# QK projection of a gated attention block: the gate's sums in another tile, raw x of the second pass loaded in other pieces, and folded router weights and u in one scratch

## The chip, the cores and the metric

The kernel runs on one core of a Trainium2 chip. Five engines work side by side, each through its own list of instructions: TensorE (PE) multiplies matrices into the banks of PSUM, ScalarE (ACT) and VectorE (DVE) read those banks and SBUF, GpSimd (POOL) does small work, and SyncE (SP) issues DMAs. SP, ACT and POOL each issue DMAs through a queue of their own. An instruction that waits holds everything behind it on its engine. The metric is the device time of one execution in microseconds, median of several runs.

## The reference, cut to what matters

`x` is 2048 tokens of 1024 features. Multi-head attention (32 heads of 32) and a sparse layer of 64 experts, chosen with two tables of 8 keys each, are mixed by a gate per token:

```python
x = A_x
g = _sigmoid((x * gate_w).sum(-1, keepdims=True))
a = _A_ref(x, A_wqkv, A_wo)      # qkv = x @ wqkv, softmax attention, @ wo
b = _B_ref(x, B_w_q, B_k1, B_k2, B_u, B_v)
return g * a + (1 - g) * b
...
# in _B_ref
q = jnp.einsum("nd,dhc->nhc", xf, w_q)
s1 = jnp.einsum("nhd,ed->nhe", q[..., :dk], k1)      # s2 with q[..., dk:] and k2
...
act = _gelu(jnp.einsum("nd,nhkd->nhk", xf, ue))      # ue = u of the best key pair
out = jnp.einsum("nhk,nhk,nhkd->nd", g, act, ve)
```

All is float32.

## The kernel before, in words

**Numbers in two parts.** Each float32 operand of a matmul is split in a rounded part *hi* (a copy on ScalarE, `hi_of`, line 135) and the rest *lo* (a subtraction on VectorE, `lo_of`, line 138). A product takes three matmuls for each 128 features: hi by hi, hi by lo, lo by hi.

**The QK projection** computes the q and k columns of `x @ wqkv` in 16 units, each with 128 columns of q and 128 of k for 1024 tokens. Pass 1 (units 0 to 7) takes tokens 1024 to 2047, pass 2 (units 8 to 15) tokens 0 to 1023, with the column chunks in reversed order, so unit 8 uses the chunk of unit 7. Half of the features (index 1 or 2) by half of the tokens makes quarters B11, B12, B21, B22 of x and A11, A12, A21, A22 of the weights. Units 0 and 8 are plain: four banks, each with 8 feature chunks by three matmuls (`plain_mm`, matmuls at line 279). The other units use Strassen's scheme with 7 products in place of 8 (`product`, line 291): P1, P5, P6, P2, P7, P3, P4 in this order, each of 12 matmuls. They need sums of quarters: T1 to T4 of x (`x_sum`, line 152, once for each pass, made in the place of a raw quarter), S1 to S4 of the weights (`w_sum`, line 222, for every unit). VectorE adds the products to the results (line 492), and `evac` turns each result, or each plain bank, into hi and lo, stores both to DRAM by DMAs on ScalarE's queue, and has ScalarE sum squares (line 245). The squares read the bank in place and come last, so they are what frees it.

**Order.** The program is written in the order of issue for each engine. Between the products, `hook(name)` runs what the table `hooks[unit, name]` holds, and `ready(name)` prepares the next unit's weights; PE's order is that of the calls. A product takes the next of six banks in turn.

**The gate.** `gate_mm` (line 190) multiplies raw x with `gate_w` into one bank; `gate_out` copies four rows of it (line 196) to the tile `zs` and sends them to DRAM, with POOL's DMAs. `zs` was a corner of the tile `rb` that also holds raw B22, and hi and lo of T3 take the slot of that tile in pass 1 (xh2) and pass 2 (xl2).

**The fold.** The router's scores are linear in x, so `w_q` is multiplied with differences of the keys once: `fold` (matmuls at line 330, two steps after most units, `wqt` being loaded pieces of `w_q`), a copy of the finished bank (line 335), then four transposes `fold_t` (line 347), a copy to the tile u7 (line 350) and a POOL DMA into the DRAM scratch WPD: 448 columns of router weights for each of 8 feature chunks.

**Pass 2's x and the router's weights.** Raw x of pass 2 is loaded by SP in units 6 and 7: B21 to the tile x8 and, as 4 pieces of 512 KB, B11 with B12 to `ra`, then B22 to `rb`. In units 14 and 15 `open_rw` reads WPD back into eight tiles wpl, and u (64 more columns) into `ugr`; `split_wp` splits them by chunk in 448 and 64 columns, and `split_n1` splits one more quarter of x, whose tile the router's own x loads (rx, on SP) follow. Then the router runs for 16 tiles of 128 tokens (24 matmuls each at line 704, a copy xu at line 708, a chain of small operations on VectorE at lines 712 to 746, eq on POOL at line 718), after it the values of attention (Strassen products at line 927), attention itself and the output.

## Time and profile before

| | |
|---|---|
| median of 3 runs | 1872.17 us (1870.14 to 1874.34) |
| profiled execution | 1873.74 us, span 1872.0 us |
| mean granted clock of PE | 0.991 |
| PE busy | 1830.5 us (98%) |
| VectorE busy | 1459.0 us (78%) |
| ScalarE busy | 1314.8 us (70%) |
| POOL busy | 174.3 us (9%) |

The span is what the profiler saw of one execution; 1.74 us of the time lie outside it. A row of a timeline gives start, duration, engine, line, operation, output<-inputs, shape and count, and in brackets the idle time of the engine ahead of it with what ended that. A row of the waits gives who waited for whom, us in total, how often and the longest. In the windows' rows the figure after POOL is the granted clock of PE, the next one the DMA share. From about 660 us to the end the kernel is attention and output, which the change leaves alone.

### The profile page before, as it was taken

How to read it: one execution, taken by the hardware profiler on the slowest of the kernel's cores; microseconds unless marked ns; L12 is line 12 of the kernel's file. 1: busy time of each engine (PE TensorE's matmuls, PEld its weight loads, DVE VectorE, ACT ScalarE, POOL GpSimd, SP SyncE). 2: the span in 40 equal slices, each digit the busy share in tenths (PEclk: the TensorE clock that was granted, in tenths of full speed). 3: DMA queues.
4: the chain of work that ended last, by engine and by line, in shares of the span. 5: the costliest groups of instructions: out<-in, count | busy, mean ns of one | idle time of the engine just before them, and what ended most of it. 6: DMA issues, size and time to landing. Idle time of an engine off the chain costs nothing.

```text
span 1872.0 us, 26493 instructions
## 1 busy us (share of the span) xinstructions
PE 1830.5 (98%) x10083; PEld 1107.3 (59%) x10083; DVE 1459.0 (78%) x1272; ACT 1314.8 (70%) x1730; POOL 174.3 (9%) x229
## 2 busy tenths in 40 slices
...
GB/s 248 203 278 248 219 208 279 252 151 177 29 118 242 231 199 169 159 181 154 179 161 183 169 173 174 170 179 164 185 170 182 151 177 171 180 158 177 286 182 57
DMA packets 136978, 344.99 MB, mean 184 GB/s; under 512 B 18320, under 2 KB 60080, under 8 KB 117712
## 3 DMA queue, kind: packets, MB, share of 16 engines
...
## 4 chain that ended last, share of the span: by engine, by line
PE 60%; issue 7%; DMA 4%; DVE 2%; POOL 2%; ACT 0%; SPq 0%; DVEq 0%; ACTq 0%; POOLq 0%
PE ring L1281 27%; PE o L1302 25%; PE pa L927 6%; PE ring L1315 1%; POOL eq L718 1%; DMA accd<-P 1%; DMA accd<-rd 1%; DMA out<-rb 1%; PE pa L1493 1%; DMA smd<-ssb 1%; SPq L76 0%; DMA t1l<-xl 0%; DVE eq L728 0%; DVE mm L725 0%; DMA V<-od 0%
## 5 line engine op out<-in xcount | busy, mean ns | idle before, releaser
L1291 ACT ACTIVATE P<-ring 128x1024 f32<-128x1024 f32 (+2 forms) x1031 | 912.9, 985 | 13.8 <-DMA accd<-P 1.0
L1331 DVE TENSOR_TENSOR acc<-acc,P 128x2048 f32<-128x2048 f32 x319 | 730.9, 2291 | 74.9 <-ACT P L1291 49.6
L1302 PE MATMUL o<-P,V 128*32 128x512 f32 x3840 | 464.8, 599 | 0.0
L1281 PE MATMUL ring<-Q,K 98*128 98x512 f32 x1024 | 272.0, 407 | 0.2
L1281 PE MATMUL ring<-z,z 98*128 98x512 f32 x1020 | 270.5, 407 | 0.6 <-ACT accd L1291 0.6
L1281 PEld LDWEIGHTS ring<-Q,K 98*128 98x128 f32 x1024 | 181.9, 188 | 144.4 <-ACT P L1291 72.6
L1281 PEld LDWEIGHTS ring<-z,z 98*128 98x128 f32 x1020 | 181.4, 188 | 142.5 <-ACT P L1291 72.4
L1302 PEld LDWEIGHTS o<-P,V 128*32 128x32 f32 x3840 | 98.8, 109 | 223.3 <-issue 214.2
L1324 POOL DMA_DIRECT2D accd<-P x95 | 81.5, 858 | 930.1 <-ACT P L1291 419.8
L1329 DVE TENSOR_TENSOR acc<-P,P 128x2048 f32<-128x2048 f32 x32 | 73.4, 2292 | 72.8 <-ACT P L1291 72.8
L291 PE MATMUL bk<-xh,S 128*128 128x512 f32 x336 | 83.2, 401 | 1.9 <-ACT bk L245 1.9
L291 PE MATMUL bk<-xh,A 128*128 128x512 f32 x336 | 82.8, 396 | 0.0
L291 PE MATMUL bk<-xl,S 128*128 128x512 f32 x336 | 82.4, 398 | 0.0
L291 PEld LDWEIGHTS bk<-xh,A 128*128 128x128 f32 x336 | 62.0, 188 | 23.8 <-issue 9.2
L291 PEld LDWEIGHTS bk<-xh,S 128*128 128x128 f32 x336 | 64.7, 194 | 16.9 <-ACT bk L245 2.4
L135 ACT ACTIVATE hi<-u 128x512 fp32r<-128x512 f32 x42 | 26.5, 632 | 68.6 <-DVE u L492 65.3
L1334 DVE TENSOR_TENSOR acc<-acc,accd 128x2048 f32<-128x2048 f32 x32 | 73.1, 2285 | 0.0
L291 PEld LDWEIGHTS bk<-xl,S 128*128 128x128 f32 x336 | 63.8, 192 | 15.4 <-issue 1.7
L1291 ACT ACTIVATE accd<-ring 128x1024 f32<-128x1024 f32 (+2 forms) x64 | 62.3, 1033 | 2.3 <-PE ring L1281 2.2
L927 PE MATMUL pa<-woh,acc 128*128 128x512 f32 x192 | 62.2, 389 | 0.0
L138 DVE TENSOR_TENSOR A<-wraw,A 128x512 fp32r<-128x512 f32 x42 | 28.9, 688 | 32.8 <-ACT A L135 32.8
L291 PE MATMUL bk<-xl,A 128*128 128x512 f32 x168 | 44.5, 417 | 8.7 <-ACT A L135 4.4
...
## 6 DMA issues: line engine op xcount, KB each, us to landing
...
```

Source lines behind the costliest of these rows:

```text
L135: nc.scalar.activation(parts[0], src, AF.Copy)
L138: nc.vector.tensor_tensor(out=parts[1], in0=src, in1=parts[0].bitcast(F32), op=OP.subtract)
L291: nc.tensor.matmul(ps, a[i][:, k, :], b[j][:, k, :], start=(k == 0 and i == j == 0), stop=(k == HC - 1 and i == 1))
L718: nc.gpsimd.tensor_tensor(out=eq, in0=eq, in1=ranks.rearrange("p c a i e -> p (c a i) e"), op=OP.mult)
L927: nc.tensor.matmul(ps, self.a[a][i][:, k, :], self.b[b][j][k], start=(not first and k == 0 and i == j == 0), stop=(k == HC - 1 and i == 1))
L1281: on_ring(nc.tensor.matmul(ring[:, i, :], K[:98, kt * 128:(kt + 1) * 128], Q[:98, qc * 512:(qc + 1) * 512], start=True, stop=True), i)
L1291: on_ring(nc.scalar.activation(P[h, kt][:, q0 * 512:(q0 + m) * 512].rearrange("p (a m) -> p a m", a=m), ring[:, i:i + m, :], AF.Exp, scale ...
L1302: nc.tensor.matmul(O[h][32 * qc:32 * qc + 32, :], Vt[g][:, kt, 32 * j:32 * j + 32], p[:, qc * 512:(qc + 1) * 512], start=(kt == 0), stop=( ...
L1324: nc.gpsimd.dma_start(ACCD[h], P[h, kt], accum_op=OP.add)
L1329: nc.vector.tensor_add(ACC[h], P[h, 0], P[h, kt])
L1331: nc.vector.tensor_add(ACC[h], ACC[h], P[h, kt])
L1334: nc.vector.tensor_add(ACC[h], ACC[h], ACCD[h])
```

## The change

1. The gate's copies go to a 128x512 tile of the pool `ev` (u2, which units use for sums), no longer to the corner of `rb`.
2. At the start of unit 1 and through unit 8, gate_out, the T4 sum, the splits of T3, T4, A12, S3, S4 and the evacuations of the plain banks stand in another order. `fold_t` moves from behind P1 to behind P5 in every unit.
3. Pass 2's raw B11 goes to x8 at (6, P5); B21 and B12 come as two loads of 1 MB into `ra` at (7, P1). hi B11 follows at (7, P6). T4 of pass 2 is made in T1's place.
4. WPD gets rows of 512 columns. A POOL DMA at the start of the program copies u (1024 rows of 64) from DRAM to its last 64 columns. `open_rw` moves to (15, P1) and loads two halves of 1 MB; the splits are two of 2048 columns on each of ScalarE and VectorE, at (15, P2) and (15, P7). `split_n1` moves behind unit 15.

ScalarE from the end of unit 0 into unit 1, before (xh_143 is the slot of `rb`, xh_407 is hi of T3 in the same slot, xh_477 hi of T4, A_421 hi of A12, S_428 and S_471 hi of S3 and S4, bk_181 to bk_184 the plain banks):

```order
L196 ACTIVATE xh_143<-bk_294 1x256 x4
L135 ACTIVATE xh_407<-xh_142 128x2048
L135 ACTIVATE A_421<-wraw 128x512
L135 ACTIVATE hi<-bk_182 128x512
L135 ACTIVATE S_428<-S_387 128x512
L496 ACTIVATE c_465<-bk_452 128x512
L245 ACTIVATE bk_182,sq<-bk_182 128x512
L76 DMA kdh<-hi 128x512
L76 DMA kdl<-lo 128x512
L135 ACTIVATE S_471<-wraw 128x512
L135 ACTIVATE hi<-bk_183 128x512
L135 ACTIVATE xh_477<-x_144 128x2048
```

and after (xh_428 is hi of T3, xh_444 of T4, A_411 of A12, S_438 and S_442 of S3 and S4, u_418 the new tile for the gate):

```order
L135 ACTIVATE A_411<-wraw 128x512
L135 ACTIVATE hi<-bk_182 128x512
L197 ACTIVATE u_418<-bk_295 1x256 x4
L135 ACTIVATE xh_428<-xh_142 128x2048
L135 ACTIVATE hi<-bk_183 128x512
L246 ACTIVATE bk_182,sq<-bk_182 128x512
L76 DMA kdh<-hi 128x512
L76 DMA kdl<-lo 128x512
L135 ACTIVATE S_438<-S_388 128x512
L135 ACTIVATE S_442<-wraw 128x512
L135 ACTIVATE xh_444<-x_144 128x2048
L502 ACTIVATE c_480<-bk_467 128x512
```

A12 and one bank's hi now stand ahead of the gate's copies and T3, the second bank's hi ahead of both S; S4 and T4 come before the second squares (not in these rows).

ScalarE from unit 8 into unit 9, before (xl_1633 is the slot of `rb`; xl_1881 hi of T3, S_1911 hi of S3, xh_1925 hi of T4, A_1952 hi of A12):

```order
L196 ACTIVATE xl_1633<-bk_1765 1x256 x4
L135 ACTIVATE xl_1881<-xh_1615 128x2048
L135 ACTIVATE hi<-bk_1754 128x512
L135 ACTIVATE S_1911<-S_1831 128x512
L135 ACTIVATE hi<-bk_1753 128x512
L245 ACTIVATE bk_1754,sq<-bk_1754 128x512
L76 DMA kdh<-hi 128x512
L76 DMA kdl<-lo 128x512
L135 ACTIVATE S_1923<-wraw 128x512
L135 ACTIVATE xh_1925<-x_1435 128x2048
L135 ACTIVATE A_1952<-wraw 128x512
L135 ACTIVATE hi<-bk_1755 128x512
```

and after (u_1873 is the tile for the gate, xl_1882 hi of T3, A_1948 hi of A12, xh_1953 hi of T4):

```order
L197 ACTIVATE u_1873<-bk_1765 1x256 x4
L135 ACTIVATE xl_1882<-xh_1609 128x2048
L135 ACTIVATE hi<-bk_1754 128x512
L135 ACTIVATE hi<-bk_1753 128x512
L246 ACTIVATE bk_1754,sq<-bk_1754 128x512
L76 DMA kdh<-hi 128x512
L76 DMA kdl<-lo 128x512
L135 ACTIVATE S_1920<-S_1831 128x512
L135 ACTIVATE A_1948<-wraw 128x512
L135 ACTIVATE S_1950<-wraw 128x512
L135 ACTIVATE xh_1953<-x_1457 128x2048
L135 ACTIVATE hi<-bk_1755 128x512
```

The second hi of a bank and the first squares move ahead of S3, and A12 ahead of S4 and T4.

VectorE in unit 15, before (wpl the loaded weights and then their lo, c and u the sums of the unit, xh_3234 the last split of x, `split_n1`):

```order
L138 TENSOR_TENSOR wpl_3121<-ugr,wph_3113 128x64
L138 TENSOR_TENSOR wpl_3122<-wpl_3122,wph_3114 128x448
L138 TENSOR_TENSOR wpl_3122<-ugr,wph_3114 128x64
L492 TENSOR_TENSOR u_3196<-c_3149,bk_3183 128x512
L492 TENSOR_TENSOR u_3197<-u_3196,bk_3162 128x512
L492 TENSOR_TENSOR c_3149<-c_3149,bk_3216 128x512
L138 TENSOR_TENSOR lo<-c_3149,hi 128x512
L95 TENSOR_TENSOR xh_3234<-x_2963,xh_3234 128x2048
L492 TENSOR_TENSOR u_3250<-u_3197,bk_3237 128x512
L492 TENSOR_TENSOR u_3196<-u_3196,bk_3237 128x512
```

and after:

```order
L498 TENSOR_TENSOR u_3161<-c_3119,bk_3148 128x512
L498 TENSOR_TENSOR u_3162<-u_3161,bk_3135 128x512
L498 TENSOR_TENSOR c_3119<-c_3119,bk_3165 128x512
L138 TENSOR_TENSOR lo<-c_3119,hi 128x512
L138 TENSOR_TENSOR wpl_3129<-wpl_3129,wph_3131 128x2048
L498 TENSOR_TENSOR u_3198<-u_3162,bk_3185 128x512
L498 TENSOR_TENSOR u_3161<-u_3161,bk_3185 128x512
L138 TENSOR_TENSOR lo<-u_3198,hi 128x512
L138 TENSOR_TENSOR wpl_3130<-wpl_3130,wph_3132 128x2048
L498 TENSOR_TENSOR u_3162<-u_3162,bk_3210 128x512
L138 TENSOR_TENSOR lo<-u_3162,hi 128x512
```

The first sums of the unit now stand ahead of the splits of the weights, which are two, and `split_n1` comes behind all of it (not in these rows).

The diff:

```diff
--- before.py
+++ after.py
@@ -49,7 +49,7 @@
     QKD = [[dram.tile([D, S], F32R, name=f"{n}d{part}") for part in "hl"] for n in "qk"]
     SHD = dram.tile([H, 2, S], F32R, name="shd")
     VD = [dram.tile([S, 512], F32, name=f"vd{i}") for i in range(2)]
-    WPD = dram.tile([128, KC, 448], F32, name="wpd")
+    WPD = dram.tile([128, KC, 512], F32, name="wpd")
     ATD = dram.tile([128, S], F32R, name="atd")
     OD = [dram.tile([128, S], F32, name=f"od{g}") for g in range(G)]
     ZD = dram.tile([1, S], F32, name="zd")
@@ -147,7 +147,7 @@
     def x_sum(p, name):
 
         a, b = dict(T1=("B12", "B11"), T3=("B22", "B12"), T2=("B22", "T1"), T4=("B21", "T2"))[name]
-        out = dict(T1="B11", T3="B12", T2="B22", T4="B21")[name]
+        out = dict(T1="B11", T3="B12", T2="B22", T4="T1" if p else "B21")[name]
         XR[name] = XR[out]
         nc.vector.tensor_tensor(out=XR[name], in0=XR[a], in1=XR[b], op=OP.subtract)
 
@@ -159,12 +159,12 @@
 
         if which == "ra":
             ra = xp.tile([128, HC, 1024], F32, name=PASS[p]["ra"])
-            XR.update(ra=ra, B11=ra[:, :, :512], B12=ra[:, :, 512:])
+            XR.update({"ra": ra, "B21" if p else "B11": ra[:, :, :512], "B12": ra[:, :, 512:]})
         elif which == "rb":
             rb = xp.tile([128, KC * 512], F32, name=PASS[p]["rb"])
-            XR.update(B22=rb[:, :2048].rearrange("p (k m) -> p k m", k=HC), zs=rb[:, 2048:2304])
+            XR["B22"] = rb[:, :2048].rearrange("p (k m) -> p k m", k=HC)
         else:
-            XR["B21"] = x8.tile([128, HC, 512], F32, name="x8")
+            XR[which] = x8.tile([128, HC, 512], F32, name="x8")
 
     def load_x(p, kc, pieces=1):
         rows, t0 = slice(kc * 128, (kc + 1) * 128), TOK0[p]
@@ -191,11 +191,12 @@
                                  start=(kc == 0), stop=(kc == KC - 1))
 
     def gate_out(p):
+        zs = ev.tile([128, 512], F32, name="u2", bufs=1)
         for q in range(4):
             row = slice(32 * q, 32 * q + 1)
-            nc.scalar.activation(XR["zs"][row, :], pz[0][row, :256], AF.Copy)
+            nc.scalar.activation(zs[row, :256], pz[0][row, :256], AF.Copy)
             c = TOK0[p] + 256 * q
-            dma(ZD[:, c:c + 256], XR["zs"][row, :], nc.gpsimd)
+            dma(ZD[:, c:c + 256], zs[row, :256], nc.gpsimd)
 
 
     def load_w(u):
@@ -372,7 +373,7 @@
             hi, lo = X[f"B{ki + 1}{n + 1}"]
             split(hi[:, k, :], lo[:, k, :], XR[f"B{ki + 1}{n + 1}"][:, k, :])
 
-    for which in ("ra", "rb", "r21"):
+    for which in ("ra", "rb", "B21"):
         x_raw_tiles(0, which)
     for name in PLAIN.values():
         w_place(name)
@@ -396,6 +397,7 @@
     for i in range(11):
         nc.tensor.matmul(b0[1, 1][:, :128], ident, ident, start=True, stop=True)
     dma(gw, ug.rearrange("p (k m) -> p k m", k=KC)[:, :, 64:65], nc.gpsimd)
+    dma(WPD[:, :, 448:], ug.rearrange("p (k m) -> p k m", k=KC)[:, :, :64], nc.gpsimd)
     dma(kraw, k12.rearrange("p (a e) -> p a e", a=2), nc.gpsimd)
     kpad_diffs()
 
@@ -432,9 +434,6 @@
             w_hi(1, "S2")
             w_lo(1, "S2")
             x_lo(0, "T2")
-            gate_out(0)
-            x_sum(0, "T4")
-            x_hi(0, "T3")
         order = [(n, i) for i in range(3) for n in range(2)]
         if kc in (0, KC - 1):
             order = [(n, i) for n in range(2) for i in range(3)]
@@ -447,15 +446,22 @@
         evac(w, CHUNK[u], TOK0[u // KC] // 512 + n, b0[w, n], b0[w, n])
 
     hooks = {}
-    w_parts(1, "A12")
+    w_hi(1, "A12")
+    w_lo(1, "A12")
     plain_evac(0, 1, 0)
+    gate_out(0)
+    x_sum(0, "T4")
+    x_hi(0, "T3")
+    x_lo(0, "T3")
+    plain_evac(0, 0, 1)
     w_hi(1, "S3")
-    x_lo(0, "T3")
+    w_sum(1, "S4")
     w_lo(1, "S3")
-    hooks[1, "P1"] = [(w_sum, 1, "S4"), (w_hi, 1, "S4"), (plain_evac, 0, 0, 1), (x_hi, 0, "T4"),
-                      (w_lo, 1, "S4")]
-    hooks[1, "P5"] = [(x_lo, 0, "T4"), (plain_evac, 0, 1, 1), (w_parts, 1, "A22")]
-    hooks[1, "P6"] = [(plain_evac, 0, 0, 0)]
+    w_hi(1, "S4")
+    x_hi(0, "T4")
+    w_lo(1, "S4")
+    hooks[1, "P1"] = [(x_lo, 0, "T4"), (plain_evac, 0, 1, 1)]
+    hooks[1, "P5"] = [(w_parts, 1, "A22"), (plain_evac, 0, 0, 0)]
     load_w(2)
     fold()
     FOLDS = {1, 2, 3, 4, 5, 6, 8, 9, 10, 11, 12, 13}
@@ -495,10 +501,10 @@
         c1 = place("c1")
         nc.scalar.activation(c1, p1, AF.Copy)
         run_late()
-        fold_t()
         hook("P1")
         ready("P1")
         p5 = product("P5")
+        fold_t()
         hook("P5")
         ready("P5")
         p6 = product("P6")
@@ -546,17 +552,20 @@
 
     def next_raw(which):
         x_raw_tiles(1, which)
-        if which == "ra":
-            for kc in range(HC):
-                load_x(1, kc)
+        if which == "B11":
+            load_quarter(0, 0, XR["B11"])
+        elif which == "ra":
+            load_quarter(0, 1, XR["B21"])
+            load_quarter(1, 0, XR["B12"])
         else:
-            load_quarter(0 if which == "r21" else 1, 1, XR["B21" if which == "r21" else "B22"])
+            load_quarter(1, 1, XR["B22"])
 
     hooks[2, "P1"] = [(w_parts, 2, "A22")]
-    hooks[6, "P1"] = [(next_raw, "r21"), (load_a21,)]
+    hooks[6, "P5"] = [(next_raw, "B11"), (load_a21,)]
     hooks[7, "P1"] = [(next_raw, "ra")]
     hooks[7, "P5"] = [(next_raw, "rb")]
-    hooks[7, "P2-"] = [(f, 1, name) for f, name in ((x_hi, "B11"), (x_lo, "B11"), (x_hi, "B21"))]
+    hooks[7, "P6"] = [(x_hi, 1, "B11")]
+    hooks[7, "P2-"] = [(x_lo, 1, "B11"), (x_hi, 1, "B21")]
     hooks[7, "P2"] = [(x_lo, 1, "B21")]
     hooks[7, "P7-"] = [(x_hi, 1, "B12")]
     hooks[7, "P7"] = [(x_lo, 1, "B12")]
@@ -589,8 +598,8 @@
     x_sum(1, "T2")
     w_lo(nxt, "S1")
     plain_group(0, 1)
+    x_hi(1, "T2")
     w_hi(nxt, "A11")
-    x_hi(1, "T2")
     x_sum(1, "T4")
     w_lo(nxt, "A11")
     w_sum(nxt, "S2")
@@ -601,19 +610,19 @@
     x_hi(1, "T3")
     plain_group(1, 0)
     plain_evac(KC, 1, 0)
+    x_lo(1, "T3")
+    plain_evac(KC, 0, 0)
     w_hi(nxt, "S3")
-    x_lo(1, "T3")
+    w_sum(nxt, "S4")
     w_lo(nxt, "S3")
-    plain_evac(KC, 0, 0)
-    w_sum(nxt, "S4")
+    plain_group(1, 1)
+    w_hi(nxt, "A12")
     w_hi(nxt, "S4")
+    w_lo(nxt, "A12")
     x_hi(1, "T4")
     w_lo(nxt, "S4")
-    plain_group(1, 1)
-    w_hi(nxt, "A12")
+    plain_evac(KC, 0, 1)
     x_lo(1, "T4")
-    w_lo(nxt, "A12")
-    plain_evac(KC, 0, 1)
     load_w(KC + 2)
     hooks[9, "P1"] = [(plain_evac, KC, 1, 1), (w_parts, nxt, "A22")]
     hooks[10, "P1"] = [(w_parts, nxt + 1, "A22")]
@@ -638,30 +647,26 @@
         wr.close()
         wqp.close()
         rw = Pool("rw", side="right")
-        wph, wpl = ([rw.tile([128, 512], F32R, name=f"wp{part}{kc}") for kc in range(KC)] for part in "hl")
-        ugr = rw.tile([128, KC, 64], F32, name="ugr")
-        Wp.extend(zip(wph, wpl))
-        rwp.extend((rw, ugr))
-        for kc in range(KC):
-            dma(wpl[kc][:, :448], WPD[:, kc, :])
-        dma(ugr, ug.rearrange("p (k m) -> p k m", k=KC)[:, :, :64])
-
-    def split_wp(*kcs):
-        for f in (hi_of, lo_of):
-            for kc in kcs:
-                for cols, src in ((slice(0, 448), Wp[kc][1][:, :448].bitcast(F32)),
-                                  (slice(448, 512), rwp[1][:, kc, :])):
-                    f([t[:, cols] for t in Wp[kc]], src)
+        wpl, wph = ([rw.tile([128, HC, 512], F32R, name=f"wp{part}{i}") for i in range(2)] for part in "lh")
+        for i in range(2):
+            dma(wpl[i], WPD[:, i * HC:(i + 1) * HC, :])
+            Wp.extend((wph[i][:, k, :], wpl[i][:, k, :]) for k in range(HC))
+        rwp.extend((rw, wph, wpl))
+
+    def hi_wp(i):
+        hi_of((rwp[1][i],), rwp[2][i].bitcast(F32))
+
+    def lo_wp(i):
+        lo_of((rwp[1][i], rwp[2][i]), rwp[2][i].bitcast(F32))
 
     hooks[14, "P1"] = [(load_n1,)]
-    hooks[14, "P4"] = [(open_rw,)]
-    hooks[15, "P1"] = [(split_wp, 0, 1)]
-    hooks[15, "P5"] = [(split_wp, 2, 3)]
-    hooks[15, "P6"] = [(split_wp, 4, 5), (split_wp, 6, 7)]
-    hooks[15, "P2"] = [(split_n1,)]
+    hooks[15, "P1"] = [(open_rw,)]
+    hooks[15, "P2"] = [(hi_wp, 0), (lo_wp, 0)]
+    hooks[15, "P7"] = [(hi_wp, 1), (lo_wp, 1)]
     for u in range(KC + 1, NUNIT):
         unit(u)
     run_late()
+    split_n1()
     rw = rwp[0]
     assert not hooks and fold_no[0] == 32 and not pending
```

## The prediction

> **What bounds the kernel now.** I read the page first, then the list of TensorE's waits, then the timelines round each place that the list names. PE is busy for 1830.5 of 1872.0 us, and the waits say where the rest of the middle goes:
>
> ```profile
> PE bk L704 <- ACT bk L245: 9.1, 1, 9.1
> PE bk L347 <- ACT x L335: 8.1, 2, 5.0
> PE bk L291 <- ACT bk L245: 5.1, 2, 3.1
> PE bk L291 <- ACT A L135: 4.4, 1, 4.4
> PE bk L279 <- DVE S L138: 3.7, 1, 3.7
> PE bk L291 <- DVE A L138: 1.2, 1, 1.2
> ```
>
> These six rows are 31.6 us, all between 40 and 411 us: four places where a pass of the QK projection begins or ends. The diff edits all four and nothing behind them. A stall also costs clock. The windows (busy time and instructions of PE, PEld, DVE, ACT, POOL, then the granted clock) show it:
>
> ```profile
> 70.00:80.00 10.00, 5.68 (x18) 4.69 (x19) 5.96 (x10) 5.68 (x14) 0.80 (x1) 0.66 1.03 273
> ```
>
> **Place 1, start of unit 1 (gate sums, T3, T4).** The timeline of PE, then ACT's and VectorE's rows that it waits for:
>
> ```profile
> 39.10 2.88 PE L291 MATMUL bk<-xl,S 128*128 128x512 f32 x12
> 41.82 2.88 PE L291 MATMUL bk<-xh,S 128*128 128x512 f32 x12
> 47.85 4.62 PE L291 MATMUL bk<-xl,A 128*128 128x512 f32 x12 [3.15 <-ACT bk L245]
> 54.41 4.60 PE L291 MATMUL bk<-xh,S 128*128 128x512 f32 x12 [1.94 <-ACT bk L245]
> 74.32 1.12 PE L347 MATMUL bk<-ident,x 128*128 128x128 f32 x4 [4.99 <-ACT x L335]
> 79.63 2.90 PE L291 MATMUL bk<-xh,S 128*128 128x512 f32 x12
> ...
> 43.14 1.91 ACT L135 ACTIVATE xh<-xh 128x2048 fp32r<-128x2048 f32 x1 [6.74 <-DMA zd<-xh]
> 53.65 0.60 ACT L245 ACTIVATE bk<-bk 128x512 f32<-128x512 f32 x1
> 73.69 0.57 ACT L335 ACTIVATE x<-bk 128x512 f32<-128x512 f32 x1
> ...
> 37.79 2.29 DVE L152 TENSOR_TENSOR x<-x,xh 128x2048 f32<-128x2048 f32 x1
> 58.63 0.68 DVE L492 TENSOR_TENSOR c<-c,bk 128x512 f32<-128x512 f32 x1
> ```
>
> A product of 12 matmuls takes 2.72 us (39.10 to 41.82); one that comes behind a wait, 4.6: each wait costs about 1.8 us beside itself. ACT stood 6.74 us because hi T3 is written into the slot from which the gate's DMAs still read. With the sums in another tile, it waits only for the T4 sum, which reads the same slot. That sum now stands behind lo A12 and one bank's lo on VectorE, so it runs from 39.0 to 41.3 instead of ending at 40.1. T3 hi starts at 41.3 (1.84 earlier). Hi of the next bank (0.5) and the first squares (0.8) end at 44.5, so P2 follows P6 at 44.6 without the 3.15.
>
> The next bank is no better off: its squares stand behind hi S3, hi S4 (after the S4 sum on VectorE, 46.6), hi T4 (1.9) and the copy c (0.5), and end at 50.4. P7 needs that bank: a wait of 3.1 instead of 1.94, and 4.6 slow, but from 50.4 instead of 54.41. P3, P4, the fold (1.9) and unit 2's P1 follow by their old spacings to 65.0.
>
> From the c sum (58.63) to the copy x for the transposes (73.69), VectorE and ACT need 15.06 us. The c sum moves to about 54.6, so the copy starts at 69.7 and ends at 70.3. The transposes now stand behind P5, which fills 65.0 to 67.7; 2.6 of the 4.99 stay, P6 starts at 71.0 and is slow. It ends at 75.6 instead of 82.37 (79.63 and 2.74): **gain 6.7 us**. If the transposes no longer wait, it is 8.5; if their wait stays whole, 5.
>
> **Places 2 and 3, the pass boundary (units 7 to 9).** SP's loads of raw x, ACT, PE and VectorE there:
>
> ```profile
> 187.39 2.90 SPq L76 DMA_DIRECT2D xh<-in_xT  x4
> ...
> 192.74 0.55 ACT L350 ACTIVATE u<-bk 128x448 f32<-128x448 f32 x1 [4.14 <-DMA xh<-in_xT]
> 200.29 1.92 ACT L135 ACTIVATE xh<-xh 128x2048 fp32r<-128x2048 f32 x1 [7.00 <-DMA xh<-in_xT]
> ...
> 215.55 4.02 PE L279 MATMUL bk<-xh,S 128*128 128x512 f32 x10 [3.65 <-DVE S L138]
> 250.56 1.22 PE L291 MATMUL bk<-xl,A 128*128 128x512 f32 x2 [4.38 <-ACT A L135]
> 256.88 5.78 PE L291 MATMUL bk<-xl,S 128*128 128x512 f32 x24
> 273.32 1.11 PE L347 MATMUL bk<-ident,x 128*128 128x128 f32 x4 [3.10 <-ACT x L335]
> 280.89 2.88 PE L291 MATMUL bk<-xl,A 128*128 128x512 f32 x12
> ...
> 219.60 2.28 DVE L152 TENSOR_TENSOR xh<-xh 128x2048 f32<-128x2048 f32 x1
> 240.26 1.92 ACT L135 ACTIVATE xl<-xh 128x2048 fp32r<-128x2048 f32 x1 [4.11 <-DMA zd<-xl]
> ```
>
> Before, hi B11 needs all four pieces of ra, 2 MB, and starts at 200.29. Now B11 comes two units ahead, hidden behind PE's work; but ACT's DMA of keys in unit 7, which goes by one semaphore with the loads, holds ACT until B21 has landed. The pieces put that landing between two rows: 0.5 MB were there 4.9 us after the issue, 2 MB after 12.9, some 5.3 us per MB, hence 195.0 for 1 MB if loads land in order; 200.3 if B21, B12 and B22 share the engines evenly. I take 196.5, nearer the first since B21 is issued first. hi B11 then starts at 197.1, 3.2 earlier, and all that follows on VectorE moves with it: lo S4 ends at 212.1 (215.5 before), and the T1 sum starts at 216.2. Place 2 gives 3.4 us. At 200.3 it gives nothing; at 195.0, 4.7, where the wait is gone.
>
> In unit 9 the gate no longer holds ACT (4.11), and hi A12 stands ahead of hi S4 and T4. By the sums of place 1, with everything 3.4 earlier: P2 follows P6 at 242.6, P7 at 245.3; P3 waits 1.9 us, until the squares of the last plain bank end at 249.5, and is slow. It starts 10.1 us before its old 259.6 (256.88 and 2.74). P4, fold, P1 and P5 run to 264.0; the copy x is ready at 263, so the transposes wait for nothing, and P2 of unit 10 starts at 267.2 instead of 280.89. **Gain of places 2 and 3: 13.7 us**, between 10 (late loads) and 18 (early loads, no wait at P3).
>
> The Trainium skill ("DMA: Bandwidth & Descriptors", section Queues, rings and completion order) says that each DMA engine consumes one queue's descriptors in ring order, but that completion is not in order per issuing engine. By ring order B21 lands first, which would be the 195.0 and a gain 1.3 us larger; the landing at 192.74 of a first piece agrees, and no row shows two whole 1 MB loads in order.
>
> **Place 4, last unit and router.**
>
> ```profile
> 398.45 2.88 PE L291 MATMUL bk<-xh,A 128*128 128x512 f32 x12
> ...
> 396.21 0.26 ACT L135 ACTIVATE wph<-ugr 128x64 fp32r<-128x64 f32 x1 [9.03 <-DMA ugr<-in_ug]
> 385.65 0.69 DVE L138 TENSOR_TENSOR A<-wraw,A 128x512 fp32r<-128x512 f32 x1 [0.44 <-ACT A L135]
> 401.67 0.68 DVE L492 TENSOR_TENSOR u<-c,bk 128x512 f32<-128x512 f32 x1
> 417.77 0.62 DVE L712 TENSOR_REDUCE m<-bk 128x64 f32<-128x448 f32 x1 [1.10 <-ACT xu L708]
> 423.83 1.92 ACT L94 ACTIVATE xh<-rx 128x2048 fp32r<-128x2048 f32 x1 [0.66 <-DMA rx<-in_xT]
> ...
> 410.39 0.80 PE L704 MATMUL bk<-wph,xh 128*128 128x512 f32 x1 [9.06 <-ACT bk L245]
> ...
> 414.94 1.05 SPq L76 DMA_DIRECT2D rx<-in_xT  x2
> 546.02 0.68 DVE L95 TENSOR_TENSOR xh<-xw,xh 128x512 fp32r<-128x512 f32 x1
> 549.47 2.89 PE L927 MATMUL bk<-xl,xh 128*128 128x512 f32 x12
> DVE mm L725 <- POOL eq L718: 10.5, 14, 1.7
> ```
>
> Before, ACT waits 9.03 us for ugr, VectorE's 16 splits end at 401.67, unit 15's sums come behind them, and PE's 9.06 us are the last bank. Now the first sums of unit 15 stand ahead of the splits. The two 1 MB loads can start only when lo A22 is done (386.3); by the two rx loads (414.94 to 423.83, 8.9 us) they land at 395.3. Hi and lo of both (2 x 1.8, 2 x 2.2) are done at 401.6, the time at which PE ends P4 (398.45 and 2.88): a wait of 0 to 1 us in place of 9.06, and no slow matmuls there.
>
> But PE is not what ends last behind it. From 417.77 to 551 VectorE goes through router and values with no wait but the 10.5 us for POOL's eq, which recur with each tile; its lo at 546.02 ends at 546.7, and the PE product that needs it starts at 549.47: 2.8 us of slack. VectorE itself gains only what rx gains: rx now waits for lo of the last x split, which moves behind unit 15's sums and ends at about 414.1, against the last squares at 414.94. So PE arrives 9 us early at values and stands there until 546.7 - 0.7. The gain is 2.8 + 0.7 = 3.5, less a slow product (1.8): **1.6 us**, from -1 (two slow products, 1 us at the splits) to 5 (no slow product, rx 1.5 earlier).
>
> **Start and the rest.** The new DMA puts 256 KB of u in 256 B pieces beside the first loads, on POOL's queue between gw and kraw. Kpad's work is first needed at 34 us, so POOL has time; the DMA engines have less, since PE waits for x and weights until some 15 us. Nearest row:
>
> ```profile
> 1.41 1.05 POOL L76 DMA_DIRECT2D gw<-in_ug  x1 [0.32 <-issue]
> ```
>
> Issuing costs POOL about 1 us. For the engines, bounds are 0 (hidden) and -2 (256 KB at the rate of the two rx loads, 4.45 us per MB, is 1.1 us; doubled for the small pieces); I take -0.7. The transposes behind P5 in the other ten units cost nothing, since PE shows no wait for them there. Copies of wq's folds into the wider scratch rows move the same bytes.
>
> Sum: 6.7 + 13.7 + 1.6 - 0.7 = 21.3 us. The profiled run took 1873.74 (span 1872.0 and 1.74 outside it), so 1852.4; the median before lies 1.57 lower, 1872.17, so **1851 us** for the median after.
>
> **Rivals.**
> - *The router takes the whole gain.* If VectorE's chain is not the limit, 9.06 and the slow first matmuls (about 1.5) are saved, 10.6 instead of 1.6: 1842. For it: the waits name PE's 9.06. Against it: VectorE's 133 us without a free gap, and 2.8 us of slack. It ends the other way only if rx lands 8 us earlier.
> - *The clock stays up over short waits.* Then P7 of unit 1, P6 of unit 2, P3 of unit 9 and the product behind the values' wait each save 1.8: 1844. Against it: 1.94 us of waiting at 54.41 were followed by 4.60. The Trainium skill ("TensorE: Matmul & The Clock Gate", section What's actually happening) has the clock halved after an idle window of about 3.4 us on a free-running count; by that rule waits of 1.9 to 3.1 us would often leave it whole, and the trace disagrees with its 1.94.
> - *The loads land late or a new wait takes unit 9.* Place 2 gives nothing, place 3 half of its 10.3, the start costs its 2: 6.7 + 5.1 + 1.6 - 2 = 11.4 us, 1861. For it: ACT now stands behind a DMA of keys for a load it does not need.
> - *Slower.* The same hold on ACT: every us that B21 lands after 200.3 delays units 7 and 8 by one. The other places give 6.7 + 10.3 + 1.6 - 0.7 = 17.9, so it decides from 218 us on, 31 us after issue, where 2 MB took 12.9. Landing at 225 gives 1879. Nothing in the rows comes near.
>
> **Chances.** The forecast 0.60; whole router gain 0.07; clock 0.06; late loads 0.19; slower 0.06; the rest (0.02) is no measurable change, which for this kernel is 0.2%, 3.7 us. All upper gains together (8.5 + 18 + 5) reach 1841, the fast rivals on top of the forecast 1842, and I go 2 us below; late loads with the low gain of places 1 and 4 (5 + 5.1 - 1 - 2 = 7.1) reach 1865. Outside that I leave about 2 in 10. Faster 0.92, same 0.02, slower 0.06.
>
> **What would show it.** In PE's waits the 9.1 on the router is under 1 and the 3.7 of L279 under 2.5; a wait of about 3 us on ACT's squares stays in unit 1; the transposes of unit 2 wait about 2.6 and those of unit 10 not at all; a new wait on VectorE's split stands in values near 525 us; ACT's idle times for zd are gone and one for raw x ends near 196. The forecast is wrong if the router's PE wait vanishes without a new one at values, if the loads in unit 7 land after 200, or if PE loses over 2 us before 30 us.

## The result, and the profile after

| | before | after |
|---|---|---|
| median, with the runs made beside it | 1871.28 us (1870.14 to 1874.34) | 1857.62 us (1856.39 to 1858.95, 4 runs) |
| profiled execution | 1873.74, span 1872.0 | 1857.74, span 1856.0 |
| mean granted clock, PE busy | 0.991, 1830.5 us | 0.994, 1826.5 us |

The ratio is 0.9925, with a 95% interval of 0.9907 to 0.9942: 14 us faster, where 21 were forecast. TensorE's waits after the change, in all, how often, and the longest:

```profile
PE bk L348 <- ACT x L336: 5.4, 3, 3.9
PE bk L292 <- ACT bk L246: 5.0, 2, 2.8
PE bk L709 <- DVEq L786: 4.8, 1, 4.8
PE pa L1491 <- ACT z L94: 4.4, 1, 4.4
PE bk L280 <- ACT xh L94: 1.5, 1, 1.5
PE bk L331 <- DMA wqt<-in_wq: 0.6, 1, 0.6
PE bk L709 <- DVE wpl L138: 0.5, 1, 0.5
```

The 9.1 at the router, the 4.4 of hi A12 and the 3.7 of the plain unit are gone. New or grown are DVEq (a branch of the program, below), z in the output (0.4 before), xh at the start and wqt in the fold.

The gain by stages comes from the start of the same instruction in the two timelines. Each number is the change of the lead over the row above. The last column takes a second profile of each program: e5_before_again, and e2_addr, which turned out to be the changed program once more (below).

| up to | before | after | gain of the stage | forecast | gain, second profiles |
|---|---|---|---|---|---|
| P1 of unit 1 | 36.21 | 38.27 | -2.1 | -0.7 | -2.1 |
| P2 of unit 2 (place 1) | 82.37 | 78.25 | +6.2 | +6.7 | +7.9 |
| P6 of unit 7 | 190.41 | 184.80 | +1.5 | 0 | +0.3 |
| P2 of unit 10 (places 2 and 3) | 280.89 | 259.08 | +16.2 | +13.7 | +13.1 |
| P4 of unit 15 | 398.45 | 379.59 | -3.0 | 0 | -0.7 |
| first product of attention (place 4) | 660.64 | 638.62 | +3.2 | +1.6 | +4.4 |
| end of the span | 1872.0 | 1856.0 | -6.0 | 0 | -5.7 |

Up to attention the change gains 22.0 us (22.9 in the second profiles) against 21.3 forecast, by terms that miss in both directions. Two profiles of the same program differ by up to 2.4 us in one stage, so a gain of 1 or 2 us in one profile says little. The last row is the surprise: 6 us go in attention and output, which the diff doesn't touch.

Place 1 in the timelines of PE, ACT and VectorE:

```profile
52.52 3.01 PE L292 MATMUL bk<-xh,S 128*128 128x512 f32 x12 [2.83 <-ACT bk L246]
72.43 1.11 PE L348 MATMUL bk<-ident,x 128*128 128x128 f32 x4 [3.90 <-ACT x L336]
73.20 5.22 PE L292 MATMUL bk<-xh,S 128*128 128x512 f32 x12
78.25 2.88 PE L292 MATMUL bk<-xl,A 128*128 128x512 f32 x12
...
43.48 1.92 ACT L135 ACTIVATE xh<-xh 128x2048 fp32r<-128x2048 f32 x1 [3.96 <-DVE x L152]
71.81 0.57 ACT L336 ACTIVATE x<-bk 128x512 f32<-128x512 f32 x1
...
41.11 2.28 DVE L152 TENSOR_TENSOR x<-x,xh 128x2048 f32<-128x2048 f32 x1
56.75 0.68 DVE L498 TENSOR_TENSOR c<-c,bk 128x512 f32<-128x512 f32 x1
```

ACT's 6.74 for the gate's DMA has become 3.96 for the T4 sum. P6 and P2 follow each other; P7 still waits 2.83 for the squares, but runs at full clock. From the c sum to the copy x are 15.06 us, the same figure as before.

The boundary of the passes, on SP, ACT and PE:

```profile
181.91 1.19 SPq L76 DMA_DIRECT2D xh<-in_xT  x2
...
187.98 0.55 ACT L351 ACTIVATE u<-bk 128x448 f32<-128x448 f32 x1 [4.85 <-PE bk L292]
188.42 1.91 ACT L135 ACTIVATE xh<-x 128x2048 fp32r<-128x2048 f32 x1
190.57 1.92 ACT L135 ACTIVATE xl<-xh 128x2048 fp32r<-128x2048 f32 x1 [0.24 <-PE bk L292]
...
202.19 3.01 PE L280 MATMUL bk<-xh,A 128*128 128x512 f32 x12
242.16 3.01 PE L292 MATMUL bk<-xl,S 128*128 128x512 f32 x12 [2.19 <-ACT bk L246]
255.85 0.66 PE L348 MATMUL bk<-ident,x 128*128 128x128 f32 x4 [0.40 <-ACT x L336]
259.08 2.88 PE L292 MATMUL bk<-xl,A 128*128 128x512 f32 x12
274.71 1.05 PE L331 MATMUL bk<-wqt,kpad 128*32 128x512 f32 x4 [0.62 <-DMA wqt<-in_wq]
325.38 0.66 PE L348 MATMUL bk<-ident,x 128*128 128x128 f32 x4 [1.14 <-ACT x L336]
```

ACT takes hi of B21 at 190.57 with no wait for its DMA, so the 1 MB issued at 181.91 had landed within 8.7 us. The plain unit has no wait at all. Two small waits follow in units 10 and 12, in a stretch in which the DMA engines are full (busy time and instructions of PE, PEld, DVE, ACT, POOL, then granted clock, DMA share, GB/s):

```profile
250.00:280.00 30.00, 28.97 (x139) 20.15 (x138) 20.41 (x32) 16.44 (x37) 0.80 (x1) 1.00 1.00 316
```

Router and values, on PE, VectorE, SP and ACT:

```profile
385.95 0.50 PE L709 MATMUL bk<-wpl,xl 128*128 128x512 f32 x1 [0.54 <-DVE wpl L138]
437.52 0.77 PE L709 MATMUL bk<-wph,xh 128*128 128x512 f32 x1 [4.77 <-DVEq L786]
527.88 2.89 PE L932 MATMUL bk<-xl,xh 128*128 128x512 f32 x12
...
437.46 0.69 DVE L751 TENSOR_REDUCE packed<-pq 128x16 f32<-128x512 f32 x1 [0.22 <-DVEq L786]
523.83 0.69 DVE L95 TENSOR_TENSOR xh<-xw,xh 128x512 fp32r<-128x512 f32 x1
...
394.68 1.30 SPq L76 DMA_DIRECT2D rx<-in_xT  x2
...
399.61 1.92 ACT L94 ACTIVATE xh<-rx 128x2048 fp32r<-128x2048 f32 x1 [3.96 <-DMA rx<-in_xT]
```

Line 786 is a branch (`tc.If`) within the router. PE stands in front of it for 4.77 us until VectorE has come there too; before, PE had no wait for the branch (VectorE was past it at 460.83, PE went on at 461.77). The wait is in all nine kernels below that have the new loads and splits (4.77 to 5.16 us), and in none of the five profiles without them.

The start, by ACT's waits for the first x, after and then before:

```profile
8.20 0.63 ACT L94 ACTIVATE xh<-xh 128x512 fp32r<-128x512 f32 x1 [2.34 <-DMA xh<-in_xT]
```

```profile
6.51 0.63 ACT L94 ACTIVATE xh<-xh 128x512 fp32r<-128x512 f32 x1 [1.02 <-DMA xh<-in_xT]
```

The output, over the first 30 us from its first product, after: PE and VectorE, and then a window with the columns as above.

```profile
1697.43 2.08 PE L1491 MATMUL pa<-woh,z 128*128 128x512 f32 x4 [4.43 <-ACT z L94]
...
1690.92 0.55 DVE L1368 RECIPROCAL rr<-rr 128x64 f32<-128x64 f32 x1 [8.00 <-DMA rr<-smd]
```

```profile
1668.90:1698.90 30.00, 25.57 (x124) 18.98 (x121) 18.53 (x27) 11.26 (x17) 3.77 (x7) 0.95 0.45 109
```

And before, VectorE and the window:

```profile
1707.85 0.55 DVE L1363 RECIPROCAL rr<-rr 128x64 f32<-128x64 f32 x1 [3.77 <-DMA rr<-smd]
```

```profile
1690.06:1720.06 30.00, 29.60 (x144) 22.33 (x141) 20.92 (x29) 12.77 (x19) 3.77 (x7) 1.00 0.54 134
```

VectorE waits 8.0 instead of 3.77 us for the sums of the last heads, PE runs dry behind it, and DMA moves 109 GB/s where it moved 134. From the first output product to the end of the span it is 187.1 us instead of 181.9.

### The profile page after: what moved, and what is told of

It reads as the page before. It is cut to its first block, busy times and chain, and to the rows that moved or that the text cites. A ratio compares the mean times of both kernels' runs of the same rounds, so it can differ in the third digit from the quotient of the medians.

```text
span 1856.0 us, 26459 instructions
## 1 busy us (share of the span) xinstructions
PE 1826.5 (98%) x10083; PEld 1106.0 (60%) x10083; DVE 1457.1 (79%) x1258; ACT 1312.7 (71%) x1716; POOL 173.6 (9%) x230
## 4 chain that ended last, share of the span: by engine, by line
PE 63%; issue 7%; DMA 2%; DVE 2%; POOL 1%; ACT 1%; SPq 0%; DVEq 0%; POOLq 0%; ACTq 0%
PE ring L1286 27%; PE o L1307 25%; PE pa L932 6%; PE pa L1491 1%; PE ring L1320 1%; PE bk L709 1%; PE pa L1498 1%; DVE acc L1336 1%; DMA smd<-ssb 1%; DMA rb<-rd 1%; POOL eq L723 1%; DMA accd<-rd 0%; DMA t1l<-xl 0%; DVE xl L95 0%; DVE xh L938 0%
## 5 line engine op out<-in xcount | busy, mean ns | idle before, releaser
L1286 PEld LDWEIGHTS ring<-Q,K 98*128 98x128 f32 x1024 | 181.9, 188 | 145.3 <-ACT P L1296 73.3
L498 DVE TENSOR_TENSOR u<-u,bk 128x512 f32<-128x512 f32 x70 | 46.6, 682 | 5.3 <-PE bk L292 2.6
```

Source lines behind the costliest of these rows:

```text
L498: nc.vector.tensor_tensor(out=out, in0=a, in1=b, op=OP.add)
L1286: on_ring(nc.tensor.matmul(ring[:, i, :], K[:98, kt * 128:(kt + 1) * 128], Q[:98, qc * 512:(qc + 1) * 512], start=True, stop=True), i)
```

## The experiments

All are the changed kernel with one edit, except where said. "Output" is the time from the first output product to the end of the span. Times of stages come from the profiled execution, medians from four or five runs; the kernel before had medians of 1871.3 to 1874.1 beside them.

| run | P1 of unit 1 | attention starts | output | median | ratio to before (95%) |
|---|---|---|---|---|---|
| before | 36.21 | 660.64 | 181.9 | 1871.28 | |
| e5_before_again (one execution) | 36.47 | 659.04 | 181.9 | 1871.78 | |
| after | 38.27 | 638.62 | 187.1 | 1857.62 | 0.9925 (0.9907 to 0.9942) |
| e1_u_late | 36.27 | 635.90 | 189.4 | 1857.15 | 0.9904 (0.9883 to 0.9926) |
| e2_addr | 38.57 | 636.19 | 186.5 | 1856.97 | 0.9915 (0.9899 to 0.9932) |
| e3_foldt_back | 37.11 | 640.60 | 186.9 | 1861.73 | 0.9940 (0.9923 to 0.9956) |
| e4_mid_fold12 | 37.73 | 635.35 | 190.6 | 1856.83 | 0.9906 (0.9890 to 0.9923) |
| e6_smd_act | 37.94 | 637.57 | 186.3 | 1855.94 | 0.9910 (0.9893 to 0.9927) |
| e7_gate_back | 37.92 | 643.58 | 187.6 | 1863.54 | 0.9952 (0.9935 to 0.9968) |
| e8_scratch_back | 36.83 | 640.13 | 181.7 | 1853.52 | 0.9903 (0.9886 to 0.9919) |
| e9_u_dma_alone | 38.32 | 642.19 | 185.8 | 1859.89 | 0.9929 (0.9907 to 0.9951) |
| e10_no_u_dma | 37.53 | 634.39 | 190.0 | 1857.20 | 0.9921 (0.9899 to 0.9943) |
| e11_best | 37.77 | 643.87 | 180.4 | 1854.84 | 0.9903 (0.9881 to 0.9924) |
| e12_rows_448 | 36.34 | 636.34 | 180.5 | 1849.19 | 0.9881 (0.9863 to 0.9898) |

**The DMA of u, issued later.**

```diff
-    dma(WPD[:, :, 448:], ug.rearrange("p (k m) -> p k m", k=KC)[:, :, :64], nc.gpsimd)
     dma(kraw, k12.rearrange("p (a e) -> p a e", a=2), nc.gpsimd)
...
     fold()
+    dma(WPD[:, :, 448:], ug.rearrange("p (k m) -> p k m", k=KC)[:, :, :64], nc.gpsimd)
     FOLDS = {1, 2, 3, 4, 5, 6, 8, 9, 10, 11, 12, 13}
```

> The new DMA of u into the scratch is issued by POOL behind unit 0 instead of at the start; nothing else differs from the changed kernel. If that DMA delays the first loads of x (my theory for P1 of unit 1 starting at 38.27 us instead of 36.21), P1 starts at 36.2 and the time falls by 2.1, to about 1855.5. If the start differs for another reason, P1 stays at 38.3 and the time at 1857.6. If 256 KB at 40 us hold up the loads of w_q there, up to 0.5 of the gain comes back as a wait on a fold.

P1 of unit 1 is back at 36.27 in this profile, 2.0 earlier, so the DMA's place costs something. Over all profiles it is less: with this DMA at the start P1 begins at 37.11 to 38.57 us (seven profiles, mean 37.98), without it at 36.21 to 37.77 (seven, mean 36.77), 1.2 us apart. ACT's second wait for x shows it without overlap: the piece is taken at 7.41 to 8.20 us with the DMA, at 6.51 to 6.78 without. Attention starts 2.7 us earlier than in the first profile of the changed kernel, but only 0.3 earlier than in its second (e2_addr). The median moves by 0.5; the output takes 2.3 more.

**The scratch declared last.**

```diff
-    WPD = dram.tile([128, KC, 512], F32, name="wpd")
+    dram.tile([128, KC, 448], F32, name="wpd_place")
...
     ZD = dram.tile([1, S], F32, name="zd")
+    WPD = dram.tile([128, KC, 512], F32, name="wpd")
```

> The scratch of 512 columns is declared last, and an unused one of 448 columns stands in its old place, so that every other DRAM scratch has the address it had before the change. Theory A: the output phase is 5 us longer after the change (187.1 us from the first output matmul to the end of the span, 181.9 before) because the shifted addresses make its DMAs slower: then it is 182 again and the time 1852.5. Theory B: that phase hangs on a chain of small DMAs whose landing depends on what else is under way at that moment: addresses change nothing, 187 or anything between 182 and 188, time 1853 to 1858.

Nothing changes, which I first read as "places in DRAM are not it". That was wrong: the places in the compiled kernel (before e12_rows_448, below) show that this edit left all of them as the changed kernel has them. The code of PE, ACT and VectorE is the same too. So the run tests neither theory; it is a second profile of the changed kernel, and shows how far two profiles of one program lie apart. In PE's rows P7 of unit 1 is slow where it was at full clock, the transposes of unit 2 wait less, and P3 of unit 9 waits longer and is slow:

```profile
52.93 4.61 PE L293 MATMUL bk<-xh,S 128*128 128x512 f32 x12 [2.81 <-ACT bk L247]
72.84 0.66 PE L349 MATMUL bk<-ident,x 128*128 128x128 f32 x4 [2.26 <-ACT x L337]
242.05 4.40 PE L293 MATMUL bk<-xl,S 128*128 128x512 f32 x12 [3.50 <-ACT bk L247]
```

The waits of units 10 and 12 (0.62 on wqt, 0.40 and 1.14 on the copy x) are absent, and attention starts 2.4 us earlier. A difference of that size between two profiles need not be the work of an edit.

**fold_t behind P1 again.**

```diff
         run_late()
+        fold_t()
         hook("P1")
         ready("P1")
         p5 = product("P5")
-        fold_t()
```

> The transposes of the fold stand behind P1 again, all else as changed. Theory: the copy x that they wait for comes when it comes, so each of the three remaining waits grows by the product that stood ahead, 2.7 us: unit 2 from 3.9 to 6.6, unit 10 from 0.4 to 3.1, unit 12 from 1.1 to 3.8; with a slow product behind each the time rises by 8 to 10 us to about 1866. Rival: the chain on ScalarE and VectorE follows PE, so that the waits hardly grow: 1858 to 1860.

The transposes of unit 2 and unit 10 in its timeline of PE:

```profile
71.37 1.12 PE L348 MATMUL bk<-ident,x 128*128 128x128 f32 x4 [6.61 <-ACT x L336]
256.57 0.66 PE L348 MATMUL bk<-ident,x 128*128 128x128 f32 x4 [3.11 <-ACT x L336]
```

Each waits 2.7 us longer than in the first profile of the changed kernel, and the median is 4.1 us higher, between the two forecasts. The wait for wqt in unit 10 and the transposes' wait in unit 12 are absent, as they are in e2_addr, so this run doesn't show that the place of `fold_t` removed them.

**The fold's middle step in unit 12 instead of 10.**

```diff
-    MID_FOLDS = {4, 10, 13}
+    MID_FOLDS = {4, 12, 13}
```

> The extra fold in the middle of unit 10 is moved to unit 12, so its 1 MB of w_q are loaded later. Theory: after the change units 9 to 12 lose 3.0 us because the DMA engines are full (share 0.99 to 1.03 from 250 to 280 us) and w_q comes late, to PE itself (0.62 us) and to ScalarE's stores, which wait for those loads (4.0 us at 324, PE then 1.14): both waits go, 1854.6. Rival: the stores wait for loads of w_q wherever the fold stands, and the wait only moves to units 12 to 14: 1857 to 1858.

Both small waits are gone and attention starts 3.3 us earlier than in the first profile of the changed kernel. But the waits are gone in e2_addr too, where the step stands in unit 10, and attention starts only 0.8 later there. So this run doesn't show that the step's place caused them. The median is 0.8 below that of the changed kernel and 0.1 below e2_addr's; the output, 190.6, is the longest of all.

**The kernel before, once more.**

> The kernel before, unchanged, for a second profile of its output phase. Theory A: that phase is 182 us long in the kernel before and 187 to 191 in all changed ones, so here 181 to 183 again. Theory B: its length varies from run to run by several us in every kernel, and the first profile was a short one: then anything from 182 to 188.

The output is 181.9 again. In unit 1 the wait for P2 was 3.14 and left the clock full (3.02 us for 12 matmuls, 4.62 in the first profile), and P7 waited 3.54 instead of 1.94: the places are the same, their split isn't.

**The last sums stored by ScalarE's queue.**

```diff
-    def norm_sums(h, ps):
+    def norm_sums(h, ps, queue=nc.sync):
...
-        dma(SMD[g][j:j + 1, :].rearrange("o (q s) -> (o q) s", q=NQ), o[::32, :])
+        dma(SMD[g][j:j + 1, :].rearrange("o (q s) -> (o q) s", q=NQ), o[::32, :], queue)
...
-            norm_sums(H - 1, sm)
+            norm_sums(H - 1, sm, nc.scalar)
```

> The changed kernel, with the last 8 KB of softmax sums (smd) stored through ScalarE's queue instead of SP's. Theory: PE's wait of 4.4 us in the output phase comes because this store is issued on SP behind 1.8 MB of loads and lands 11.2 us later; on ScalarE's queue it goes out 2.6 us earlier, at 6.4 us of that phase instead of 9.0, and lands in under 6 us: the wait goes and the phase falls from 187 to 183, the time to 1853.5. Rival: the DMA engines themselves are full, whatever the queue; the store lands as late, and the time stays at 1857.

VectorE's wait for rr falls from 8.00 (5.74 in e2_addr) to 3.93, yet the output is only 0.8 shorter than in the first profile of the changed kernel and 0.2 shorter than in e2_addr. The late store isn't what makes the output long.

**The gate's sums back in the corner of rb.**

```diff
-            XR["B22"] = rb[:, :2048].rearrange("p (k m) -> p k m", k=HC)
+            XR.update(B22=rb[:, :2048].rearrange("p (k m) -> p k m", k=HC), zs=rb[:, 2048:2304])
...
-        zs = ev.tile([128, 512], F32, name="u2", bufs=1)
+        zs = XR["zs"]
```

> The gate's sums are written to the corner of rb again, all else as changed. Theory: hi T3 waits again for the gate's DMAs: in unit 1 until 46.2 us instead of 43.5, so P2 and P7 start 2.7 later; in unit 9, where the copies end at 225.0 and the DMAs need some 7 us, it starts at 232 instead of 225.2, 6.7 later, and PE with it. Sum +9 to +12 with slow products: 1867 to 1870. Rival: the new order alone does the work (squares and A12 ahead of T3 and S4), and the tile matters little: under +4, 1861.

ACT's rows at the splits of T3, in units 1 and 9:

```profile
46.16 1.91 ACT L135 ACTIVATE xh<-xh 128x2048 fp32r<-128x2048 f32 x1 [6.85 <-DMA zd<-xh]
230.75 1.92 ACT L135 ACTIVATE xl<-xh 128x2048 fp32r<-128x2048 f32 x1 [4.47 <-DMA zd<-xl]
```

The waits for zd are back, and attention starts 5.0 us later, the median is 5.9 higher, between the two forecasts. So the other tile is worth some 5 us of the 22 at places 1 and 3. In unit 1 the loss is the one I forecast: the transposes start 37.19 us after P1, against 34.15 to 34.36 in the ten kernels with the new tile and `fold_t` behind P5. Unit 9 loses less than the 6.7; I put that down to the next waits (squares, copy x), which were already near, and no run tests it.

**Part 4 undone** (448 columns, ugr and eight loads, 32 splits, `split_n1` in unit 15, no DMA of u: the functions `open_rw` and `split_wp` and the hooks as in the lines with a minus in the change's diff).

> Scratch of 448 columns, u loaded by itself, eight loads and 32 splits at their old places, and the last x split in unit 15: part 4 of the change undone, all else as changed. Theory: the router's first matmul falls back by the 9.2 us that it had gained, but attention begins only 3.2 us later, since VectorE sets the router's pace up to the branch; the start gains back 2.1 us; so attention starts 1.1 later (639.7) and the time is 1858.7. Rival: PE's 9.06 us were a true loss: attention starts 7 later, 1864.

```profile
389.89 0.79 PE L712 MATMUL bk<-wph,xh 128*128 128x512 f32 x1 [9.57 <-ACT bk L246]
```

The 9.57 at the router are back, the wait at the branch is gone, and attention starts at 640.13, as forecast (639.7). From P4 of unit 15 to attention it takes 262.7 us, as before the change (262.2), where the changed kernel takes 259.0: the gain of place 4 is part 4's. But the kernel is 4.1 us **faster** than the changed one, since the output is 181.7. So part 4 costs the 5 us there. Two runs split it.

**The DMA of u alone; and everything of part 4 but that DMA.** The first is e8_scratch_back with these lines:

```diff
-    WPD = dram.tile([128, KC, 448], F32, name="wpd")
+    WPD = dram.tile([128, KC, 512], F32, name="wpd")
...
+    dma(WPD[:, :, 448:], ug.rearrange("p (k m) -> p k m", k=KC)[:, :, :64], nc.gpsimd)
...
-            dma(wpl[kc][:, :448], WPD[:, kc, :])
+            dma(wpl[kc][:, :448], WPD[:, kc, :448])
```

> Part 4 is undone but for the DMA of u into the scratch, whose rows are 512 wide again; what it writes is not read (u comes by its own load, as before). Two theories for the output phase (from the first output matmul pa<-z,z to the end of the span), which took 181.7 to 181.9 us without part 4 and 186.3 to 190.6 with it. First: the one DMA more on GpSimd's queue, by which every later DMA is counted on another semaphore; then the phase is 186 or longer here, P1 of unit 1 starts near 38.3 instead of 36.8, and the median is 1.5 + 5 above the 1853.5 of the kernel without part 4, about 1860. Second: the new loads and splits at the router; then only the start is paid, the phase stays at 181.8 and the median is about 1855.

The second is the changed kernel with these:

```diff
-    dma(WPD[:, :, 448:], ug.rearrange("p (k m) -> p k m", k=KC)[:, :, :64], nc.gpsimd)
...
+        ugr = rw.tile([128, KC, 64], F32, name="ugr")
         for i in range(2):
-            dma(wpl[i], WPD[:, i * HC:(i + 1) * HC, :])
+            dma(wpl[i][:, :, :448], WPD[:, i * HC:(i + 1) * HC, :448])
...
+        dma(ugr, ug.rearrange("p (k m) -> p k m", k=KC)[:, :, :64])
...
+    def wp_cols(f, i):
+        rw, wph, wpl, ugr = rwp
+        for cols, src in ((slice(0, 448), wpl[i][:, :, :448].bitcast(F32)),
+                          (slice(448, 512), ugr[:, i * HC:(i + 1) * HC, :])):
+            f([t[i][:, :, cols] for t in (wph, wpl)], src)
```

> The changed kernel without the DMA of u into the scratch: u is loaded into a tile of its own at (15, P1), behind the two halves, and each half is split in two pieces, 448 and 64 columns wide; order and places of loads and splits are the new ones. First theory (the DMA): P1 of unit 1 at 36.5 instead of 38.3, attention begins about 2 us before the 638.6 of the changed kernel, the output phase is 181.8, median about 1851. Second theory (loads and splits at the router): the start as in the first, but the phase 186 or longer, median about 1856. In both, the wait at the router's branch (4.8) stays within 1 us.

The first alone would speak for the DMA of u (1859.89, output 185.8), the second alone for the loads and splits (1857.2, output 190.0); together they let both theories fall, since neither part is needed for the long output. What both have is the scratch of 512 columns. The places (bytes) of some DRAM tensors in the compiled kernels:

```
tensor   before, e8, e11, e12      e10         after, e2, e9
zd                 81920         81920         2179072
wpd             33644544      33644544           81920
shd             35479552      35741696        35741696
od0             54878208      55140352        55140352
rd              55959552      56221696        56221696
smd7            63758336      64020480        64020480
```

In each of the nine kernels with the long output everything from shd on lies 256 KB further (262144 bytes). The scratch declared last (e2_addr) changed none of these against the changed kernel: its unused tensor takes no place.

**One number: rows of 448 in e10_no_u_dma.**

```diff
-    WPD = dram.tile([128, KC, 512], F32, name="wpd")
+    WPD = dram.tile([128, KC, 448], F32, name="wpd")
...
-            dma(wpl[i][:, :, :448], WPD[:, i * HC:(i + 1) * HC, :448])
+            dma(wpl[i][:, :, :448], WPD[:, i * HC:(i + 1) * HC, :])
```

> The run without the DMA of u (e10_no_u_dma), its scratch rows back at 448 columns, and nothing else: every instruction, load and semaphore is as there. The two runs before showed that neither the DMA of u alone nor the loads and splits alone explain the long output phase, since each of them has it (185.8 and 190.0). What the kernels with a long phase share, and the three without lack, is the scratch of 2 MB in place of 1.75 MB: every DRAM tensor that is placed behind it (the attention's scratch rd, the outputs od of the heads, the sums smd) lies 256 KB further on. The kernel with the scratch declared last did not test this, since its unused tensor took no place and the places of the others, from shd on, were those of the changed kernel. If the places are the cause: attention starts at 634.4 as in the run without the DMA, the output phase is 181.8 instead of 190.0, the median is 8 us below its 1857.2, about 1849, the fastest of all. If the cause is anything in the loads and splits at the router: phase 188 or longer, median 1857.

1849.19 us, as expected, 8.0 below its twin; the ranges of the two (1847.78 to 1851.08 and 1856.81 to 1859.78) lie apart. Attention starts at 636.34 instead of the 634.4 expected, within the spread of two profiles of one program, and is 1.9 us shorter. VectorE's row for rr and the window of the first 30 us of output, first both with rows of 512, then both with 448:

```profile
1687.27 0.55 DVE L1375 RECIPROCAL rr<-rr 128x64 f32<-128x64 f32 x1 [7.77 <-DMA rr<-smd]
```

```profile
1665.49:1695.49 30.00, 25.90 (x124) 19.27 (x121) 18.55 (x27) 11.49 (x18) 3.78 (x7) 0.94 0.45 109
```

```profile
1683.06 0.55 DVE L1375 RECIPROCAL rr<-rr 128x64 f32<-128x64 f32 x1 [3.49 <-DMA rr<-smd]
```

```profile
1665.55:1695.55 30.00, 30.00 (x146) 22.77 (x143) 20.93 (x29) 13.31 (x20) 3.78 (x7) 1.00 0.51 140
```

The same instructions start the output at the same time, and DMA moves 140 instead of 109 GB/s. It begins in the last heads: in ACT's exponentials, some 997 us after the start of attention, a wait stands with rows of 512 that is absent with 448 (where 12 follow without a gap).

```profile
1624.03 6.97 ACT L1303 ACTIVATE P<-ring 128x1536 f32<-128x1536 f32 x7
1632.07 3.77 ACT L1303 ACTIVATE P<-ring 128x512 f32<-128x512 f32 x4 [1.07 <-PE ring L1293]
```

```profile
1624.57 11.36 ACT L1303 ACTIVATE P<-ring 128x512 f32<-128x512 f32 x12
```

In e9_u_dma_alone, at the same place, the row names the transfer: POOL's DMA that adds P to accd has not done with the tile that ACT is to write.

```profile
1639.03 3.77 ACT L1300 ACTIVATE P<-ring 128x512 f32<-128x512 f32 x4 [1.02 <-DMA accd<-P]
```

The other profiles say the same. The wait at 997 us (1.02 to 1.21 us) is in all nine kernels with the shift and in none of the five profiles without it. In the first 30 us of output DMA moves 126 to 140 GB/s without the shift, 109 to 122 with it. POOL issues seven loads of od at the start of the output, the last of them 3.6 us in: it lands 9.1 to 9.9 us after its issue without the shift, 10.8 to 13.8 with it. Nor is it the chip: e5 and e8 were short and e6 and e7 long on one chip, e11 short and e9 and e10 long on another.

Since the scratch isn't read again behind unit 15, more than 1,200 us earlier, what stays is the places of the tensors behind it. Which of them (rd, od, smd) meets what in the memory was not told apart: the slow loads of od run beside those of rd.

**Part 4 undone, and the fold's middle step in unit 12.** The edits of e8_scratch_back and e4_mid_fold12 together.

> Part 4 undone, and the fold's middle step of unit 10 moved to unit 12, by which the waits of 0.62 on wqt and 1.14 on the copy x went away in the changed kernel (3.3 us less up to attention, though only 0.8 at the end). If those 0.8 came from part 4's longer output phase, which is not here, attention starts at 636.8 instead of 640.1, the phase is 181.8 and the median is 1850.2. If the moved step itself lengthens the output phase (190.6 there, the longest of all), the phase is 184 or longer and the median 1852 to 1854.

A miss: the output is short (180.4), so the moved step doesn't lengthen it, but attention starts at 643.87. P1 of unit 1 is 0.9 us later than in e8_scratch_back, and P3 of unit 9 waits 3.42 and is slow (4.61) where it waited 2.33 at full clock (3.01): 0.9 + 1.1 + 1.6 is 3.6 of the 3.7. The moved step gains nothing that stands out from this.

## Why the prediction was right or wrong

**The result lies in the range, and the sign and the main mechanism hold;** the number is 6.6 us too low, for a reason that the prediction didn't have. That the sum up to attention fits within 2 us is in part luck: its terms miss by up to 3 us and cancel. And two of the prediction's own signs of being wrong came up: the router's wait vanished without a new one at values, and PE lost over 2 us before 30 us (its first gate matmul starts at 28.92 instead of 26.85).

**Place 1, 6.7 forecast, 6.2 measured (7.9 in the second profiles).** The order of the rows came as worked out: P6 and P2 without a wait, P7 2.83 against 3.1, the 15.06 from the c sum to the copy x. The step "a wait of 3.1 [...] and 4.6 slow" failed in its second half: P7 took 3.01. It was no gain, because ACT sets the time: the transposes wait 3.90 instead of the 2.6, and P6 behind them is slower (5.22). Over eleven kernels with this order and the new tile, P7 waited 2.79 to 2.84; it ran at full clock in four and slow (4.24 to 4.62) in seven, and in the ten with `fold_t` behind P5 the transposes start 34.15 to 34.36 us after P1 in either case.

**The clock rival was half right.** I let each wait of 1.9 us and more cost 1.8. Waits of 2.19 (P3 of unit 9) and 2.83 left the clock full, 3.90, 4.43 and 4.77 did not, and 1.94 in the profile of before came right behind another wait, 3.15. The Trainium skill ("TensorE: Matmul & The Clock Gate", section What's actually happening) describes a free-running window of about 3.4 us that has to pass idle before the clock is halved. That one wait of 2.8 ends both ways agrees with a free-running count, and not with my fixed price; that seven of eleven such waits cost clock although they are shorter than the window does not agree with the figure, taken strictly. Shorter ones disagree as well: behind the transposes' waits of 2.26 to 2.48 us in unit 2, P6 ran at full clock in three kernels (3.00 to 3.02) and slow in four (4.40 to 4.59).

**Places 2 and 3, 13.7 forecast, 16.2 measured (13.1 in the second profiles).** The step that failed is "ACT's DMA of keys in unit 7 [...] holds ACT until B21 has landed". ACT issues the keys at 187.05, has hi B11 at 188.42 and takes B21 at 190.57 with no wait for a DMA. The landing itself, 9.1 us after the issue by my figures, was under 8.7. So the plain unit waits for nothing (I left 0.3), and unit 9 starts earlier by more. P3 waits 2.19, near the forecast 1.9, and at full clock (+1.6), which is luck of this profile: in eight of the other ten kernels it waits 3.11 to 3.63 and is slow (4.24 to 5.49). The transposes wait 0.40 instead of 0.

**"The transposes behind P5 in the other ten units cost nothing" and the silence on units 10 to 15: -3.0 (-0.7 in the second profiles), and +1.5 (+0.3) in units 2 to 7.** In unit 10 the fold now comes when DMA is full (share 1.00, 316 GB/s) and waits 0.62 for wqt; in unit 12 the transposes wait 1.14. So the step "cost nothing" failed in this profile. But e2_addr, the same program, has neither wait: the loss comes and goes from one execution to the next, and no run shows an edit that removes it.

**Place 4, 1.6 forecast, 3.2 measured (4.4 in the second profiles).** "PE arrives 9 us early at values and stands there" was right that PE can't keep the 9.06, and wrong on the place: it meets VectorE at the branch within the router, and waits 4.77 there. "VectorE itself gains only what rx gains" held, but the term was mis-sized: counted from P4 of unit 15, rx was forecast 0.7 us earlier and comes 5.4 earlier, 4.0 of it since it landed 4.9 us after the issue instead of 8.9; why it landed sooner, no run shows. VectorE reaches values 22.2 us earlier (546.02 to 523.83), so PE has no wait at 525. The rival with the whole router gain fell: the 9.06 are gone, 4.77 and some slow matmuls came.

**The start, -0.7 forecast, -2.1 measured.** The second profiles give -2.1 as well. Of this the DMA's place explains 1.2 us on the mean of seven profiles each, between my -0.7 and my bound of -2; the rest lies within the spread of the starts.

**Attention and output, 0 forecast, -6.0 measured (-5.7 in the second profiles).** "From about 660 us to the end the kernel is attention and output, which the change leaves alone" holds for the instructions and not for the time. I had read "Copies of wq's folds into the wider scratch rows move the same bytes" as a reason to cost the wider scratch at nothing; its price was not in its copies but in where it puts what lies behind it. With the old size, and without the DMA of u, the loads and splits at their new places give 1849.19: 22.1 us faster than the kernel before in the same runs (1871.26), and 8.4 faster than the changed kernel.
